# Gates' logits in four parts and sinkhorn's steps in another order, in a kernel of delta-rule attention, a Mish layer and a sinkhorn-gated expert layer

## The chip, the core and the metric

The kernel runs on one core of a Trainium2 chip. The core has TensorE (matmuls, with a sequence of weight loads beside them), VectorE, ScalarE, GpSimd and SyncE (which issues the DMAs here); in profiles they are PE, PEld, DVE, ACT, POOL and SP. Each works off its own queue in order, and semaphores tie the queues together. PSUM holds matmul results, SBUF the rest.

The metric is the device time of one execution in microseconds, as a median of runs. The median before is 2372.52 us (three runs, 2372.46 to 2373.16).

## The reference, cut to what matters

```python
def _moe2_ref(x, w_gate, w1, w2):              # x: 3072 tokens of 384
    logits = x @ w_gate                        # 8 experts
    logits = logits - logits.max()
    P = np.exp(logits)
    for _ in range(8):                         # sinkhorn
        P /= P.sum(1, keepdims=True) + 1e-09
        P /= P.sum(0, keepdims=True) + 1e-09
        P *= N / E
    for e in range(E):
        h = np.maximum(x @ w1[e], 0.0)         # 384 -> 1024
        ye = h @ w2[e]                         # 1024 -> 384
        out += P[:, e:e + 1] * ye
```

Ahead of it stand a delta-rule attention over 768 positions (`y[t] = q[t] S`, then a rank-1 update of S for each of 32 heads) and a layer of 2048 hidden units with the Mish activation. All is float32; the large matmuls are done in three passes of split operands (high x high, high x low, low x high).

## The kernel before, in words

**First stage.** Tokens come in six blocks (c = 0 to 5) of 512. In each block, 16 units of the Mish layer are followed by 8 units of expert 0: `for f in range(U1, NU)`, f = 16 to 23, called s16 to s23. Meanwhile the attention of the next blocks is spread over the units by a table (`PLACES`, `window`), and its elimination steps on VectorE are handed out by `fill` and by `tick`, which runs behind every operation called through `vec` (all of these have line 458 in the profile).

**Second stage.** Experts 1 to 7 go over the six blocks in units of 128 hidden features, block 5 first (`for u in range(N1, N + 2)`; unit v = u - N1 counts from 0).

**A unit.** `e_first` is the first matmul of a unit: nine 512-column matmuls into a PSUM tile `psh`. `e_relu` makes two SBUF tiles of it: `hh` (ScalarE, relu of `psh`) and `hl` (VectorE, what `hh` lost in rounding). `e_second` (called by `y0_second` and `o_second`) multiplies them with the second weights, twelve 384-column matmuls, and runs two units behind its `e_first`. `hh` and `hl` have two buffers each, so the `hh` of a unit can be written when the `e_second` of the unit two before has read its own. In the first stage `e_relu(u - 1)` is called in unit u, in the second stage `e_relu(u)`.

**Weights.** `conversions` splits the next weights: a ScalarE copy (line 251) and a GpSimd subtraction (line 252), at the end of a unit. Every sixth unit of the second stage, from v = 3, `x2_split` does the same with a block's tokens (lines 1189 and 1190).

**Gates.** `logits(c)` multiplies a block's tokens `xr` with the gates' weights: 4 token tiles x 3 products in float32, recorded as 24 matmuls of 8 columns, and one VectorE copy into `lg`. It is called in unit s17, in the last block in s16.

**Sinkhorn.** `lg` holds all logits, then P, as 128 x 24 x 8. `sink_start` finds the maximum over partitions by a transpose and a product on TensorE and takes exp by way of a sigmoid. `sink_round` is five VectorE operations (lines 352 to 356): row sums, + 1e-9, reciprocal, multiply, column sums over the 24. `sink_round_end` is a product with a matrix of ones on TensorE (line 360), which adds the column sums over the partitions, and four VectorE operations (lines 362 to 365): + 1e-9, reciprocal, scale, multiply. `sink_step` takes the next one of a list of 18 (`sinks`). In the last block it is called twice a unit from s17 on, ahead of `e_second` and behind it; in the second stage once between `e_first` and `e_relu` and once behind `e_second`. Units 0 and 1 of the second stage take the last four steps. The PSUM tiles of these products come from `bank()`, two buffers that the second stage's odd units share. When the list is empty, `P` scales the accumulators of expert 0, one tile a unit (line 1251).

The order on every engine is that of the code (`manual_schedule`).

Of the kernel before, what the change touches and what calls it, by code (L numbers as in the profile page):

```python
# [13 lines left out]
ALU = mybir.AluOpType  # L14
# [70 lines left out]
def delta_mish_sinkhorn_kernel(  # L85
# [246 lines left out]
    P = lg  # L332
    Pf = lg.rearrange("p t e -> p (t e)")

    def sink_start():
        m1, m2, m3 = sk["m"][:, 0:1], sk["m"][0:1, 1:2], sk["m"][:, 2:3]
        nc.vector.tensor_reduce(out=m1, in_=Pf, axis=AX.X, op=ALU.max)
        ps = small[0]()
        nc.tensor.transpose(ps[0:1, 0:128], m1, id_sb)
        nc.vector.tensor_reduce(out=m2, in_=ps[0:1, 0:128], axis=AX.X, op=ALU.max, negate=True)  # L340
        ps2 = small[0]()[:, 0:1]
        mm(ps2, lhsT=sk["ones"][0:1, :], rhs=m2, start=True, stop=True)
        nc.vector.tensor_copy(m3, ps2)
        nc.scalar.activation(out=Pf, in_=Pf, func=AF.Sigmoid, bias=m3)
        d = sk["d"]
        nc.vector.tensor_scalar(out=d, in0=Pf, scalar1=-1.0, scalar2=1.0, op0=ALU.mult, op1=ALU.add)
        nc.vector.reciprocal(out=d, in_=d)
        nc.vector.tensor_tensor(out=Pf, in0=Pf, in1=d, op=ALU.mult)
# [15 lines left out]
        nc.vector.tensor_scalar(out=cr, in0=cr, scalar1=float(NTOK) / E, scalar2=None, op0=ALU.mult)  # L364
        nc.vector.tensor_tensor(out=P, in0=P, in1=cr[:, None, :].to_broadcast([128, NT, E]), op=ALU.mult)

    sinks = deque([sink_start, lambda: None] + [sink_round, sink_round_end] * ROUNDS)

    def sink_step():
        if sinks:  # L370
            sinks.popleft()()
# [6 lines left out]
    with ExitStack() as p1:  # L378
# [474 lines left out]
            if c < NBLK - 1:  # L853
                nc.sync.dma_start(out=x2_dram[c], in_=xr)

        def logits(c):
            ps = bank()[:, 0:4 * E].rearrange("p (t e) -> p t e", e=E)
            for t in range(4):
                for k in range(KD):
                    mm(ps[:, t, :], lhsT=xr[:, k, t * 128:(t + 1) * 128], rhs=wg_sb[:, k, :], start=(k == 0), stop=(k == KD - 1))  # L860
            vec.tensor_copy(lg[:, 4 * c:4 * c + 4, :], ps)


        def fill(us):
# [175 lines left out]
        def window(c):  # L1040

            pe = {m: [] for m in MARKS}
            rest = {m: [] for m in MARKS}
            late = {m: [] for m in MARKS}
            nxt, far = c + 1, c + 2
            rest[f"s{U1 + (c < NBLK - 1)}"].append(lambda: logits(c))
            if c == 0:
                for t in (2, 3):
                    pe["s1"].append(lambda t=t: st_s(0, t))
                for t in range(4):  # L1050
                    rest[f"s{t + 1}"].append(lambda t=t: prep_v(1, t))
                for i in range(8):
                    rest[f"s{i + 2}"].append(lambda t=i // 2, w=1 + i % 2: mask_p(1, t, (w,)))
            if nxt < NBLK:
                m0, at = PLACES[c][0:2]
                rest[MARKS[m0]].append(drain_elim if c else lambda: elim1(60, nc.vector))
                rest[MARKS[m0]].append(lambda: st_lane_out(nxt))
                for hf in range(2):
                    late[MARKS[m0 + 1]].append(lambda hf=hf: st_m1(nxt, hf))
                    rest[MARKS[m0 + 2]].append(lambda hf=hf: st_place(nxt, hf, (0, 2)))  # L1060
                    late[MARKS[m0 + 2]].append(lambda hf=hf: st_m2(nxt, hf))
                ch = chain_list(nxt)
                assert len(at) >= len(ch)
                for p, stage in zip(at, ch):
                    pe[MARKS[p]].append(stage)
            if far < NBLK:
                sq0, mb0, at, kq0, kt0, eq0 = PLACES[c][2:]
                if c == 0:
                    rest["s2"].append(lambda: load_kt(far))
                    rest["s2"].append(lambda: load_vt(far))  # L1070
                if far + 1 < NBLK:
                    rest[MARKS[kt0]].append(lambda: load_kt(far + 1))
                    rest[MARKS[kt0]].append(lambda: load_vt(far + 1))
                for t in range(4):
                    rest[MARKS[sq0 + t // 2]].append(lambda t=t: prep_sq(far, t))
                rest[MARKS[sq0 + 1]].append(lambda: prep_pow(far, ALL))
                rest[MARKS[sq0 + 3]].append(lambda: [op() for op in norm_ops(far, ALL)])
                rest[MARKS[kq0]].append(drain_decode)
                for t in range(4):
                    rest[MARKS[kq0]].append(lambda t=t: load_kq(far, t))  # L1080
                    rest[MARKS[mb0[t]]].append(lambda t=t: prep_mb(far, t, nc.gpsimd))
                    for hf in range(2):
                        pe[MARKS[at[2 * t + hf]]].append(lambda t=t, hf=hf: st_g(far, t, hf, True))
                    rest[f"s{U1 + t + 4}"].append(lambda t=t: prep_v(far, t))
                rest[MARKS[eq0]].append(lambda: eq.extend(lane_in_ops(far) + elim_ops(far)))
            return pe, rest, late

        with tc.manual_schedule():
            banks[:] = [0, [A1, A1]]
            for c in range(NBLK):  # L1090
# [50 lines left out]
                for f in range(U1, NU):  # L1141
                    u = b + f
                    posts = side_pe(f"s{f}", 0)
                    ready(u)
                    e_first(u, ps_h, mi_p, x1h, x1l)
                    if f > U1:
                        e_relu(u - 1)
                    side_rest(f"s{f}", posts)
                    if f > U1:
                        fill(3.6 if c == 0 else 3.2)  # L1150
                    if c == NBLK - 1 and f > U1:
                        sink_step()
                    if f > U1 + 1:
                        y0_second(u - 2)
                    if c == NBLK - 1 and f > U1:
                        sink_step()
                    conversions(u)
                e_relu(b + NU - 1)
                split = [lambda kc=kc: st_x1(c + 1, kc) for kc in range(KD)] if c + 1 < NBLK else []
# [58 lines left out]
    with tc.manual_schedule():  # L1218
# [10 lines left out]
        for u in range(N1, N + 2):  # L1229
            v = u - N1  # L1230
            if u < N:
                e, c, f = info(u)
                e_first(u, *[(ps_h, mi_p), (ps_a, mi_p)][v % 2], *xs[c], *[("h",), ("a",)][v % 2])
                sink_step()
                e_relu(u)
            if v >= 2:
                o_second(u - 2)
            sink_step()
            if u < N:
                conversions(u)  # L1240
            if v >= 3 and (v - 3) % 6 == 0 and (v - 3) // 6 < NBLK - 1:
                c = (v - 3) // 6
                x2_split(c)
                if c + 2 < NBLK - 1:
                    x2_load(c + 2)
                if c + 1 < NBLK - 1:
                    acc_load(c + 1)
            if not sinks and todo:
                c, t = todo.popleft()
                a = acc[c][:, t, :]  # L1250
                nc.vector.tensor_scalar(out=a, in0=a, scalar1=P[:, 4 * c + t, 0:1], scalar2=None, op0=ALU.mult)
# [63 lines left out]
```

## Time and profile before

| | |
|---|---|
| median of three runs | 2372.52 us |
| the profiled execution, whole | 2370.98 us |
| its span, first to last instruction | 2369.2 us |
| TensorE busy | 2298.2 us, 97% of the span |
| VectorE, ScalarE, GpSimd busy | 34%, 24%, 20% |
| granted TensorE clock, mean | 0.971 of full speed |

Busy shares are an average over unlike stages. The first stage ends and the second begins at 949.6 us; sinkhorn runs from 914.8 to 959.0 us. In the second stage TensorE is busy without a break from 964 us to the end. What a change there is worth is read from the stretch itself: which wait of TensorE ends last, and at which clock its matmuls run.

### The profile page before, as it was taken

Reading aid. Unit: us, or ns where it says so; the run is one execution under the profiler, and the core shown is the slowest. Engines: PE = TensorE matmul, PEld = TensorE weight load, DVE = VectorE, ACT = ScalarE, POOL = GpSimd, SP = SyncE. Lnnn points to the kernel's source line nnn. Section 1 sums busy time; section 2 is a strip of 40 time slices with the busy share of each in tenths; the row PEclk is TensorE's granted clock in tenths of the full one; section 3 lists DMA queues with packets and bytes.
Section 4 is the critical chain, followed back from the end, with each engine's and each line's share of the span. In section 5 each row is a group of like instructions: output and inputs, shape, how many; then the busy total and the mean of one; then the engine's idle time right before and its main releaser. Section 6 shows DMA issues by size and latency. Waiting matters only on the chain.

```text
span 2369.2 us, 36112 instructions
## 1 busy us (share of the span) xinstructions
PE 2298.2 (97%) x15492; PEld 1992.1 (84%) x15492; DVE 801.2 (34%) x1369; ACT 559.9 (24%) x999; POOL 471.2 (20%) x370
## 2 busy tenths in 40 slices
PE   8688899999999999999999999999999999999998
PEld 4477778878788888899999999999999999999998
DVE  8884725527162104431222222222222122212222
ACT  5244332332323232211211211121121111112111
POOL 5686442341412121310200100020020011001000
PEclk6799999999999999999999999999999999999999
DMA  5357643637344454410100100010010001000111
GB/s 173 134 195 211 211 154 129 211 114 238 131 164 148 162 198 140 167 40 1 54 1 1 37 17 1 1 54 1 1 54 1 1 20 34 1 1 27 27 27 27
DMA packets 79727, 196.00 MB, mean 83 GB/s; under 512 B 7696, under 2 KB 50448, under 8 KB 79568
## 3 DMA queue, kind: packets, MB, share of 16 engines
q1 hardware_dynamic: 79568, 193.70, 24.8%
q8 instruction: 122, 2.00, 0.3%
q14 instruction: 37, 0.30, 0.0%
HBM read 161.43 MB, written 32.24 MB: 82 GB/s over the span
## 4 chain that ended last, share of the span: by engine, by line
PE 90%; DVE 6%; DMA 2%; POOL 1%; issue 1%; ACT 0%; SPq 0%; DVEq 0%; POOLq 0%; ACTq 0%
PE psh L299 42%; PE o L321 30%; PE x L840 8%; PE y L321 3%; DVE t L635 1%; DVE lane L641 1%; PE psa L590 1%; PE psa L729 1%; PE psa L763 1%; DVE lane L623 1%; PE psa L711 1%; PE psa L860 1%; PE psa L747 1%; PE psa L677 1%; DMA wd<-w 0%
## 5 line engine op out<-in xcount | busy, mean ns | idle before, releaser
L299 PE MATMUL psh<-xh,w 128*128 128x512 f32 x2052 | 662.7, 404 | 13.7 <-DMA w<-wd 6.7
L314 DVE SCALAR_TENSOR_TENSOR hl<-psh,hh 128x512 fp32r<-128x512 f32 x384 | 265.1, 690 | 1111.8 <-ACT hh L313 1111.7
L313 ACT ACTIVATE hh<-psh 128x512 fp32r<-128x512 f32 x384 | 229.7, 598 | 1312.1 <-PE o L321 1154.5
L299 PEld LDWEIGHTS psh<-xh,w 128*128 128x128 f32 x2052 | 381.1, 191 | 91.2 <-issue 12.2
L299 PE MATMUL psh<-xl,w 128*128 128x512 f32 x1026 | 412.0, 402 | 4.2 <-DVE xl L458 4.2
L321 PE MATMUL o<-w,hh 128*128 128x384 f32 x1584 | 405.5, 337 | 0.0
L321 PEld LDWEIGHTS o<-w,hh 128*128 128x128 f32 x1584 | 288.2, 188 | 19.8 <-issue 4.9
L321 PE MATMUL o<-wx,hh 128*128 128x384 f32 x1104 | 282.0, 336 | 0.0
L321 PE MATMUL o<-w,hl 128*128 128x384 f32 x792 | 267.0, 337 | 0.0
L299 PE MATMUL psh<-xh,wx 128*128 128x512 f32 x828 | 258.3, 393 | 0.0
L299 PEld LDWEIGHTS psh<-xl,w 128*128 128x128 f32 x1026 | 196.3, 191 | 51.2 <-DVE xl L458 5.9
L321 PEld LDWEIGHTS o<-wx,hh 128*128 128x128 f32 x1104 | 201.5, 188 | 13.1 <-issue 2.1
L829 POOL TENSOR_TENSOR gl<-x,gh 128x512 fp32r<-128x512 f32 x96 | 127.5, 1328 | 420.0 <-ACT gh L828 416.2
L252 POOL TENSOR_TENSOR w<-raw,w 128x768 fp32r<-128x768 f32 x41 | 75.7, 1848 | 669.9 <-ACT w L251 669.8
L321 PE MATMUL o<-wx,hl 128*128 128x384 f32 x552 | 186.0, 337 | 0.0
L299 PEld LDWEIGHTS psh<-xh,wx 128*128 128x128 f32 x828 | 153.5, 188 | 25.2
L299 PE MATMUL psh<-xl,wx 128*128 128x512 f32 x414 | 163.4, 395 | 0.0
L840 PE MATMUL x<-gh,w 128*128 128x512 f32 x576 | 150.7, 397 | 0.0
L321 PEld LDWEIGHTS o<-w,hl 128*128 128x128 f32 x792 | 148.6, 188 | 0.0
L840 PEld LDWEIGHTS x<-gh,w 128*128 128x128 f32 x576 | 107.5, 189 | 24.9
L252 POOL TENSOR_TENSOR wx<-raw,wx 128x768 fp32r<-128x768 f32 x23 | 42.4, 1845 | 399.7 <-ACT wx L251 399.7
L321 PEld LDWEIGHTS o<-wx,hl 128*128 128x128 f32 x552 | 103.6, 188 | 0.0
(165 smaller groups left out, 2358.2 us busy)
## 6 DMA issues: line engine op xcount, KB each, us to landing
w<-wd SPq DMA_DIRECT2D x120, 768.0 KB, 4.4
raw<-in_w_dram SPq DMA_DIRECT2D x128, 192.0 KB, 2.6
wd<-w SPq DMA_DIRECT2D x24, 768.0 KB, 4.3
kq<-in_qkb_dram SPq DMA_DIRECT2D x20, 256.0 KB, 6.9
vt<-in_vtok_dram SPq DMA_DIRECT2D x6, 768.0 KB, 8.6
kq<-in_w_in_dram SPq DMA_DIRECT2D x12, 384.0 KB, 4.7
kq<-in_w_out_dram SPq DMA_DIRECT2D x12, 384.0 KB, 5.6
y0d<-xr SPq DMA_DIRECT2D x6, 768.0 KB, 4.7
```

The lines of the kernel that those rows point to most:

```text
L252: nc.gpsimd.tensor_tensor(out=w[:, 1], in0=r, in1=w[:, 0].bitcast(F32), op=ALU.subtract)
L299: mm(ps, lhsT=wi(u, pw, kc), rhs=(xh, xl)[px][:, kc, :], start=(n == 0), stop=(n == 3 * KD - 1))
L313: nc.scalar.activation(out=h, in_=ps, func=AF.Relu)
L314: nc.vector.scalar_tensor_tensor(out=l, in0=ps, scalar=0.0, in1=h.bitcast(F32), op0=ALU.max, op1=ALU.subtract)
L321: mm(o[t], lhsT=(h, l)[ph][:, t * 128:(t + 1) * 128], rhs=wo(u, pw, 0, DM), start=(f == 0 and n == 0), stop=(f == U2 - 1 and n == 2))
L590: mm(ps[0:64, :, i], lhsT=k[64:64 + D, 0, h, :], rhs=k[64:64 + D, 0:2, h, :], start=True, stop=True)
L623: + [(1.14, lambda p=p: nc.vector.transpose(out=lane[p:p + 32], in_=v[p:p + 32, 32:64, :])) for p in (32, 96)]
L635: eng[0].tensor_tensor(out=slot[0], in0=lane[:, s + 1:32, s:s + 1].to_broadcast([128, n, s]), in1=lane[:, s:s + 1, 0:s].to_broadcast([128, ...
L641: eng[0].tensor_tensor(out=lane[:, s + 1:32, 0:s], in0=lane[:, s + 1:32, 0:s], in1=slot[0], op=ALU.add)
L677: mm(ps[p + 32:p + 64, i], lhsT=g[p:p + 32, t, h, 32:64], rhs=t11[p:p + 32, b, :], start=True, stop=True)
L829: nc.gpsimd.tensor_tensor(out=l, in0=p, in1=h.bitcast(F32), op=ALU.subtract)
L840: mm(x2ps[c][k], lhsT=wo(u, pw, k * 128, k * 128 + 128), rhs=(h, l)[pg], start=(f == 0 and n == 0), stop=(f == U1 - 1 and n == 2))
```

## The change

Two things are changed.

`logits` takes a token tile t and makes one of four parts: 6 of the 24 matmuls, into a PSUM tile of its own, and a copy of 8 columns. The parts are called in four units in a row, s17 to s20, in the last block s16 to s19.

The list of steps has 22 entries: the local maximum, the transpose with the maximum over partitions, and the rest of the start are steps of their own, with empty steps between. `sink_step` is called twice in a row, in the last block from s19 on, ahead of `e_second`; in the second stage behind `e_relu` and ahead of `e_second`. With that a unit holds the end of one round and then the next round's sums, and the product with the ones stands a unit behind the sums that it reads. Two rounds are ended in the last block, six in units 0 to 5 of the second stage.

```diff
+    def sink_max():
+        nc.vector.tensor_reduce(out=sk["m"][:, 0:1], in_=Pf, axis=AX.X, op=ALU.max)
+
+    def sink_max_all():
+        ps = small[0]()
+        nc.tensor.transpose(ps[0:1, 0:128], sk["m"][:, 0:1], id_sb)
+        nc.vector.tensor_reduce(out=sk["m"][0:1, 1:2], in_=ps[0:1, 0:128], axis=AX.X, op=ALU.max, negate=True)
+
     def sink_start():
-        m1, m2, m3 = sk["m"][:, 0:1], sk["m"][0:1, 1:2], sk["m"][:, 2:3]
-        nc.vector.tensor_reduce(out=m1, in_=Pf, axis=AX.X, op=ALU.max)
-        ps = small[0]()
-        nc.tensor.transpose(ps[0:1, 0:128], m1, id_sb)
-        nc.vector.tensor_reduce(out=m2, in_=ps[0:1, 0:128], axis=AX.X, op=ALU.max, negate=True)
+        m2, m3 = sk["m"][0:1, 1:2], sk["m"][:, 2:3]
...
-    sinks = deque([sink_start, lambda: None] + [sink_round, sink_round_end] * ROUNDS)
+    none = lambda: None
+    sinks = deque([sink_max, none, sink_max_all, none, sink_start] + [sink_round, sink_round_end] * ROUNDS + [none])
...
-        def logits(c):
-            ps = bank()[:, 0:4 * E].rearrange("p (t e) -> p t e", e=E)
-            for t in range(4):
-                for k in range(KD):
-                    mm(ps[:, t, :], lhsT=xr[:, k, t * 128:(t + 1) * 128], rhs=wg_sb[:, k, :], start=(k == 0), stop=(k == KD - 1))
-            vec.tensor_copy(lg[:, 4 * c:4 * c + 4, :], ps)
+        def logits(c, t):
+            ps = bank()[:, 0:E]
+            for k in range(KD):
+                mm(ps, lhsT=xr[:, k, t * 128:(t + 1) * 128], rhs=wg_sb[:, k, :], start=(k == 0), stop=(k == KD - 1))
+            vec.tensor_copy(lg[:, 4 * c + t, :], ps)
...
-            rest[f"s{U1 + (c < NBLK - 1)}"].append(lambda: logits(c))
+            for t in range(4):
+                rest[f"s{U1 + (c < NBLK - 1) + t}"].append(lambda t=t: logits(c, t))
...
-                    if c == NBLK - 1 and f > U1:
+                    if c == NBLK - 1 and f > U1 + 2:
+                        sink_step()
                         sink_step()
                     if f > U1 + 1:
                         y0_second(u - 2)
-                    if c == NBLK - 1 and f > U1:
-                        sink_step()
...
+                e_relu(u)
                 sink_step()
-                e_relu(u)
+                sink_step()
             if v >= 2:
                 o_second(u - 2)
-            sink_step()
```

VectorE's queue in the second stage. Before, from the end of round 7 in unit 0 on (the round with its line 356, then `hl` of unit 1, then the end of round 8):

```order
L365 TENSOR_TENSOR lg<-lg,gate 128x192
L352 TENSOR_REDUCE gate<-lg 128x24
L353 TENSOR_SCALAR gate<-gate 128x24
L354 RECIPROCAL gate<-gate 128x24
L355 TENSOR_TENSOR lg<-lg,gate 128x192
L356 TENSOR_REDUCE gate<-lg 128x8
L314 SCALAR_TENSOR_TENSOR hl<-psh,hh 128x512
L362 TENSOR_SCALAR gate<-psa 128x8
L363 RECIPROCAL gate<-gate 128x8
L364 TENSOR_SCALAR gate<-gate 128x8
```

After, unit 2 of the second stage, between the last row of unit 1 and the first of unit 3 (the lines are four higher: 360 is the column sums, 366 to 369 the end of a round):

```order
L360 TENSOR_REDUCE gate<-lg 128x8
L314 SCALAR_TENSOR_TENSOR hl<-psh,hh 128x512
L366 TENSOR_SCALAR gate<-psa 128x8
L367 RECIPROCAL gate<-gate 128x8
L368 TENSOR_SCALAR gate<-gate 128x8
L369 TENSOR_TENSOR lg<-lg,gate 128x192
L356 TENSOR_REDUCE gate<-lg 128x24
L357 TENSOR_SCALAR gate<-gate 128x24
L358 RECIPROCAL gate<-gate 128x24
L359 TENSOR_TENSOR lg<-lg,gate 128x192
L360 TENSOR_REDUCE gate<-lg 128x8
L314 SCALAR_TENSOR_TENSOR hl<-psh,hh 128x512
```

Before, the round stood ahead of its unit's `hl`; now `hl` comes first, then the end of the round before, then the next round.

TensorE's queue in the second stage, unit 3. Before, `e_first` (`psh`) is followed by `e_second` (`o`):

```order
L299 MATMUL psh<-xl_1199,wx_8591 128x512
L299 MATMUL psh<-xh_1198,wx_8591 128x512 x2
L299 MATMUL psh<-xl_1199,wx_8591 128x512
L321 MATMUL o_8694<-w_86,hh 128x384 x2
L321 MATMUL o_8694<-w_86,hl 128x384
```

After, at the same place, with the product with the ones (`gate`) between them:

```order
L299 MATMUL psh<-xl_1199,wx_8588 128x512
L299 MATMUL psh<-xh_1198,wx_8588 128x512 x2
L299 MATMUL psh<-xl_1199,wx_8588 128x512
L364 MATMUL psa<-gate 128x8
L321 MATMUL o_8701<-w_86,hh 128x384 x2
L321 MATMUL o_8701<-w_86,hl 128x384
```

Before, units 0 and 1 alone had such a product, behind their `e_first`; now units 0 to 5 have one, and from unit 2 on it stands ahead of an `e_second`.

TensorE's queue in block 4, units s17 to s18, the logits (`psa<-wg_sb,xr`). Before:

```order
L299 MATMUL psh<-xh_1198,w_1200 128x512 x2
L299 MATMUL psh<-xl_1199,w_1200 128x512
L860 MATMUL psa<-wg_sb,xr 128x8 x12
L299 MATMUL psh<-xh_1198,w_85 128x512 x2
L299 MATMUL psh<-xl_1199,w_85 128x512
```

After, from the same matmul on:

```order
L299 MATMUL psh<-xh_1198,w_1200 128x512 x2
L299 MATMUL psh<-xl_1199,w_1200 128x512
L865 MATMUL psa<-wg_sb,xr 128x8 x3
L299 MATMUL psh<-xh_1198,w_85 128x512 x2
L299 MATMUL psh<-xl_1199,w_85 128x512
L299 MATMUL psh<-xh_1198,w_85 128x512 x2
L299 MATMUL psh<-xl_1199,w_85 128x512
L299 MATMUL psh<-xh_1198,w_85 128x512 x2
L299 MATMUL psh<-xl_1199,w_85 128x512
L865 MATMUL psa<-wg_sb,xr 128x8 x3
L321 MATMUL y_7650<-w_89,hh 128x384 x2
```

The lump of twelve products is now three, and three more follow behind each of the next three units' `e_first`.

## Rows read from the trace of the kernel before

**Rows 1.** TensorE's timeline, second stage: start us, us, line, operation, tiles, shape, count, [idle].
```profile
957.34 0.60 PE L360 MATMUL psa<-gate 128*128 128x8 f32 x2 [3.16 <-DVE gate L356]
957.79 1.20 PE L299 MATMUL psh<-xh,w 128*128 128x512 f32 x2
...
961.33 0.52 PE L321 MATMUL o<-w,hh 128*128 128x384 f32 x2
...
963.43 0.63 PE L299 MATMUL psh<-xh,wx 128*128 128x512 f32 x2
...
965.53 0.51 PE L321 MATMUL o<-w,hh 128*128 128x384 f32 x2
```

**Rows 2.** Timeline of TensorE, last block: products of sinkhorn's start and first round.
```profile
916.70 0.38 PE L342 MATMUL psa<-gate 1*128 1x1 f32 x2 [0.37 <-DVE gate L340]
...
922.23 0.39 PE L360 MATMUL psa<-gate 128*128 128x8 f32 x2 [0.75 <-DVE gate L356]
```

**Rows 3.** Waits of TensorE's weight loads, 900 to 965 us: total us, times, longest.
```profile
PEld psa L360 <- DVE gate L356: 5.4, 4, 3.6
```

**Rows 4.** Stretches: from:to, length, each engine's busy us (count), PEclk, DMA share, GB/s.
```profile
237.14:243.97 6.83, 6.83 (x36) 5.63 (x33) 1.17 (x3) 2.35 (x5) 5.03 (x7) 0.50 0.58 175
...
810.56:813.97 3.41, 3.41 (x11) 3.02 (x10) 0.00 (x0) 0.00 (x0) 0.00 (x0) 0.50 0.92 386
913.88:917.00 3.12, 2.75 (x14) 1.96 (x13) 1.32 (x4) 0.00 (x0) 0.00 (x0) 1.00 0.00 0
957.36:960.77 3.41, 3.41 (x9) 2.83 (x10) 1.85 (x6) 0.00 (x0) 1.07 (x1) 0.50 1.00 401
```

**Rows 5.** Timeline of TensorE, block 4: the logits and units beside them.
```profile
806.63 2.74 PE L860 MATMUL psa<-wg_sb,xr 128*128 128x8 f32 x24
809.22 0.71 PE L299 MATMUL psh<-xh,w 128*128 128x512 f32 x2
...
815.06 0.63 PE L299 MATMUL psh<-xh,w 128*128 128x512 f32 x2
```

**Rows 6.** Timeline of VectorE, block 1: the copy of the logits.
```profile
397.14 0.19 DVE L458 COPY lg<-psa 128x32 f32<-128x32 f32 x1 [3.25 <-PE psa L860]
```

**Rows 7.** Timeline of TensorE, block 1: second unit after the logits.
```profile
403.30 0.73 PE L299 MATMUL psh<-xh,w 128*128 128x512 f32 x2 [0.34 <-DVE hl L314]
```

**Rows 8.** Timeline of ScalarE, second stage.
```profile
963.46 0.60 ACT L313 ACTIVATE hh<-psh 128x512 fp32r<-128x512 f32 x1 [7.64 <-PE o L321]
965.54 0.85 ACT L251 ACTIVATE wx<-raw 128x768 fp32r<-128x768 f32 x1 [1.48 <-DMA raw<-in_w_dram]
```

**Rows 9.** Timeline of VectorE, last block and second stage.
```profile
920.35 0.34 DVE L352 TENSOR_REDUCE gate<-lg 128x24 f32<-128x192 f32 x1
...
953.12 0.15 DVE L362 TENSOR_SCALAR gate<-psa 128x8 f32<-128x8 f32 x1
...
954.14 0.35 DVE L352 TENSOR_REDUCE gate<-lg 128x24 f32<-128x192 f32 x1
...
955.08 1.68 DVE L355 TENSOR_TENSOR lg<-lg,gate 128x192 f32<-128x192 f32 x1
...
964.09 0.69 DVE L314 SCALAR_TENSOR_TENSOR hl<-psh,hh 128x512 fp32r<-128x512 f32 x1 [3.48 <-ACT hh L313]
964.70 0.41 DVE L1251 TENSOR_SCALAR acc<-acc,lg 128x384 f32<-128x384 f32 x1
...
973.06 1.64 DVE L1251 TENSOR_SCALAR acc<-acc,lg 128x384 f32<-128x384 f32 x1
```

**Rows 10.** VectorE's operations on lg: count, ns min/median/max, first, last start.
```profile
L355 DVE TENSOR_TENSOR lg<-lg,gate x8: 357/358/1675, 921.3 to 955.1; 128x192 f32<-128x192 f32 x8
```

**Rows 11.** Timeline of GpSimd, second stage.
```profile
954.74 3.69 POOL L252 TENSOR_TENSOR wx<-raw,wx 128x768 fp32r<-128x768 f32 x2 [11.07 <-ACT wx L251]
...
969.05 1.96 POOL L252 TENSOR_TENSOR wx<-raw,wx 128x768 fp32r<-128x768 f32 x1 [0.73 <-ACT wx L251]
970.96 3.52 POOL L1190 TENSOR_TENSOR xl<-x2r,xh 128x1536 fp32r<-128x1536 f32 x1
```

## The prediction, made before the changed kernel ran

> **What bounds the kernel now.** I read TensorE's timeline first. In the second stage a unit is one `e_first` (nine 512-column matmuls), 965.53 - 963.43 = 2.10 us, and one `e_second`, 963.43 - 961.33 = 2.10 us, back to back: 4.20 us with TensorE never idle [rows 1]. So a microsecond that TensorE loses is lost, and what other engines do counts only where TensorE waits for it or where its clock falls. The change touches two places where that happens. The first are sinkhorn's products with the ones matrix, which wait for VectorE's column sums: 0.75 us at 922.23 in the last block and 3.16 us at 957.34 in the second stage [rows 1, 2]; the waits of their weight loads come to 5.4 us, 3.6 of them at 957.34, and the product after the maximum adds 0.37 us [rows 2, 3]. The second is the clock: granted at 0.50 of full speed (1.2 instead of 2.4 GHz) for 6.83 us after the logits of block 0, for 3.41 us after those of block 4, and for 3.41 us after the 3.16 us wait; after the logits of block 5 it stayed at 1.00 [rows 4].
>
> **Logits in four parts.** The 24 matmuls of 8 columns take 809.22 - 806.63 = 2.59 us in a lump; a part is a quarter, 0.65 us, and the four sum to the same. What can change is the clock behind them and who waits for whom.
> Block 4: from the end of the lump to the end of the unit's `e_second` pass 815.06 - 809.22 = 5.84 us, where a unit takes 4.20 [rows 5]. Nothing waits there, so the clock costs 1.64 us. Parts of 0.65 us, each amid 4.2 us of full matmuls, should not lower it: -1.6 us.
> Blocks 1 to 3 are different. VectorE sits idle for 3.25 us until the logits come, copies them at 397.14, then works off elimination steps, and `hl` behind them releases TensorE only at 403.30, after a wait of 0.34 us [rows 6, 7]. That is 6.2 us behind the copy, against 4.20 of matmuls, so the clock there costs nothing. With the split the copy of the first part lands 1.94 us sooner and so does 403.30; the second part lies in TensorE's wait, the third and fourth cost 0.65 us each. 1.94 - 1.30 = 0.65 us a block, -1.9 us in three.
> Block 0: 6.83 us at half clock, 3.4 us lost at most, but the chunks' small matmuls stand there too and can lower the clock by themselves: between 0 and -3.4, I take -1.6. Together **-5.1 us**, bounds 0 and -10 (the latter if the third and fourth parts were hidden too).
>
> **The sinkhorn steps.** The products keep their number (eight, plus two for the maximum). New is the order: in every unit `e_relu`, then the product and VectorE's four operations of a round's end, then the next round's five. The product of a unit needs the sums that VectorE made in the unit ahead. In the last block that works: `e_relu` there serves the unit before, whose buffers are free at the unit's start. In the second stage, to which six products now fall instead of two, `e_relu` serves the unit itself, and it is now ahead of the round in VectorE's queue. Its ScalarE half `hh` waits for the buffer that `e_second` of two units before still reads: it starts at 963.46, 0.03 us after that `e_second` is over at 963.43, having waited 7.64 us [rows 1, 8]. VectorE's `hl` follows at 964.09 and the next operation in its queue at 964.70 [rows 9]. So behind the end of a unit come: 1.27 us to the end of `hl`; the four operations, 954.14 - 953.12 = 1.02; the five to the product, 922.23 - 920.35 = 1.88 [rows 2, 9]. The sums are there 4.17 us into the next unit, and TensorE wants them after its `e_first`, at 2.10. **Each product of the second stage whose predecessor unit had an `e_second` waits at least 2.07 us.** Queued behind it on TensorE is the `e_second`, and with that the buffer for the next `hh`, so nothing catches up.
> GpSimd makes this longer. The weight conversions put a subtraction of 1.9 us on it, and VectorE operations that read only SBUF are held until it ends: the round's multiply at 955.08 took 1.68 us where the median of the eight is 0.358 [rows 9, 10], while the GpSimd operations begun at 954.74 ran [rows 11]; the scale of an accumulator at 973.06 took until 974.70, and GpSimd's 3.52 us from 970.96 end at 974.48 [rows 9, 11]. The multiply of a round's end works on the same tiles, `lg` and `gate`, so I take it to be held as well; `hl`, which reads PSUM, I take to be free. The Trainium skill ("SBUF — State Buffer", section "Who interferes with whom") has the rule behind it: a VectorE instruction with two SBUF inputs is blocked for the whole of a GpSimd instruction that reads SBUF, if that began first. By that rule the multiply of a round's end is held too, which no run of it shows; without it the sum below is about 1 us less, as the next multiply is held in its stead.
> Unit by unit:
> Last block, unit 22 (first round's product): from the product of the maximum to the first sums pass 922.23 - 916.70 = 5.53 us, less one `hl` of 0.61: 4.92 [rows 2, 9]. TensorE covers two halves of 2.10 and the product of some 0.3, 4.5: a wait of 0.4 us. But two conversions are queued on ScalarE right behind the sigmoid, and their GpSimd operations can hold two of VectorE's for up to 1.96 each: between 0.4 and 4.3, I take 2.7, since the first is met part way.
> Second stage, unit 1: the same order and the same GpSimd operation as now at 955.08, so the 3.16 us and the low clock stay: 0. Unit 2: the sums come about 3.5 us behind the product of unit 1, and `e_first` at the low clock takes 961.33 - 957.79 = 3.54 [rows 1]: 0; at full clock a wait of 1.0 would replace the 1.44 us of clock.
> Unit 3: the conversion waits for its weights until 965.54, 2.1 us into its unit [rows 8]; with 0.85 for the copy GpSimd runs from about 3.0 to 4.9 and holds the round's multiply, so the sums come at 5.7: wait 3.6.
> Unit 4: GpSimd starts 1.42 us into the unit (969.05, where the unit starts at 965.53 + 2.10 = 967.63), and right behind it runs the 3.52 us split, to 6.9 [rows 11]. The third operation of the end (at about 1.7) is held to 3.4, the fourth by the split to 6.9, then 0.2 and 1.88: 9.0, wait 6.9.
> Unit 5: one conversion: third operation held to 3.4, sums at 5.9, wait 3.8.
> New waits: 2.7 + 3.6 + 6.9 + 3.8 = 17.0. Clock: after 3.16 us of idling `e_first` took 3.54 instead of 2.10, 1.44 lost [rows 1, 4]; three of the new waits are longer, the one of 2.7 I count half: 3.5 x 1.44 = 5.0. Gone are the waits of the last block, 5.4 - 3.6 + 0.4 = 2.2 [rows 2, 3]. Sum **+19.8 us**. Bounds: +6 (GpSimd's holds half as long, the clock never falling) to +23.
> Later work: the accumulators' scaling starts four units later and still ends a unit ahead of the first sum into each. SP's queue and DMA issues are unchanged.
>
> **Sum.** 19.8 - 5.1 = +14.7 us. The profiled execution took 2370.98 us (span 2369.2), 1.54 under the median of 2372.52; 2370.98 + 14.7 = 2385.7 by the profile, **2387.2 us** by the median.
>
> **Rivals.** (a) GpSimd's operations miss VectorE's. Then the waits are 0.4 and three times 2.07, unit 2 waits 1.0, unit 1 only 2.07 instead of 3.16 and the clock stays up (-1.44): 0.4 + 6.2 + 1.0 - 1.1 - 1.4 - 2.2 - 5.1 = -2.2, 2370.3 us. For it: half a microsecond of shift can let an operation slip through. Against it: the conversions come in every unit from 0 to 5, behind the same `hh` as VectorE's work. 10%.
> (b) The change does what it says and no product waits: -(3.16 + 1.44 + 2.2 + 5.1) = -11.9, 2360.6 us. It needs `hl` not to stand ahead of the round, or `hh` not to wait for `e_second`; the orders and [rows 8] say both do. 3%. It decides if the sums come less than 2.10 us into a unit.
> (c) The lump of logits never cost any clock, the low stretches have another cause and stay. Then 1.6 + 1.6 us of the gain go: 2390.4 us. 5%. The Trainium skill ("TensorE: Matmul & The Clock Gate", section "HAM oscillation — how this bites in real kernels") ties the fall to idle gaps of TensorE, and the lump has none; the 0.50 behind it in two blocks [rows 4] speaks against that reading.
> (d) In blocks 1 to 3 three more copies, each with an elimination step called behind it, delay `hl`: 0.6 us in nine units and 1.44 us of clock in three, +9.7: 2396.9 us. Against it: a unit with a logits part is 4.85 us long, enough for the 0.6 us more. 10%.
>
> **How the numbers follow.** The forecast, with its bounds mostly between 2378 and 2394, has 72%; (a) 10, (b) 3, (c) 5, (d) 10. The range 2377 to 2395 holds the forecast, (c) and the milder half of (d). Measurements here tell 0.2%, 4.7 us, from no change: slower than 2377.3 are the forecast, (c), (d): 87%; within are (a)'s: 10%; faster (b)'s: 3%.
>
> **What would show it.** In the profile after: products of the second stage waiting for VectorE in units 1, 3, 4 and 5 (3.2, 3.6, 6.9, 3.8 us), none after; `hl` ahead of a round each time; multiplies held 1.5 to 3.5 us; granted clock 0.50 behind these waits and 1.00 behind the logits of block 4; blocks 1 to 3 shorter by 0.65 us each. It is wrong if `hh` starts ahead of the end of `e_second`, or if the waits stay near 2 us.

## The result and the profile after

The changed kernel takes **2389.77 us** (median of six executions, 2384.70 to 2399.84), the kernel before 2372.32 us beside it (six, 2370.71 to 2373.16). The ratio is 1.0078, 95% interval 1.0057 to 1.0100: slower by more than the noise, where 2387.2 was forecast in a range of 2377 to 2395. The profiled execution of the changed kernel, 2384.70 us (span 2382.6), was the fastest of its six, so the traces are 13.7 us apart and the medians 17.5.

TensorE's timeline of the changed kernel, all products that wait, from the last block (932.47) to unit 5 of the second stage (986.85), answers [rows 1, 2]:

```profile
932.47 0.39 PE L364 MATMUL psa<-gate 128*128 128x8 f32 x2 [2.40 <-DVE gate L360]
...
952.81 0.39 PE L364 MATMUL psa<-gate 128*128 128x8 f32 x2 [3.16 <-DVE gate L360]
...
956.25 0.39 PE L364 MATMUL psa<-gate 128*128 128x8 f32 x2 [0.85 <-DVE gate L360]
...
964.29 0.39 PE L364 MATMUL psa<-gate 128*128 128x8 f32 x2 [3.37 <-DVE gate L360]
...
976.93 0.60 PE L364 MATMUL psa<-gate 128*128 128x8 f32 x2 [6.41 <-DVE gate L360]
...
986.85 0.39 PE L364 MATMUL psa<-gate 128*128 128x8 f32 x2 [2.98 <-DVE gate L360]
```

The waits of the same products between 900 and 1000 us (total, times, longest) answer [rows 3]:

```profile
PEld psa L364 <- DVE gate L360: 21.8, 6, 6.8
PE psa L364 <- DVE gate L360: 19.2, 6, 6.4
```

What makes unit 4's 6.41 us long stands in three timelines, which answer [rows 8, 9, 11]. ScalarE's, `hh` of that unit:

```profile
968.19 0.60 ACT L313 ACTIVATE hh<-psh 128x512 fp32r<-128x512 f32 x1 [6.58 <-PE o L321]
```

VectorE's, the multiply of unit 3's round, then `hl` of unit 4 and the end of a round behind it:

```profile
961.89 1.81 DVE L359 TENSOR_TENSOR lg<-lg,gate 128x192 f32<-128x192 f32 x1
...
968.82 0.69 DVE L314 SCALAR_TENSOR_TENSOR hl<-psh,hh 128x512 fp32r<-128x512 f32 x1 [4.58 <-ACT hh L313]
...
969.85 1.60 DVE L368 TENSOR_SCALAR gate<-gate 128x8 f32<-128x8 f32 x1
971.49 3.53 DVE L369 TENSOR_TENSOR lg<-lg,gate 128x192 f32<-128x192 f32 x1
```

GpSimd's, a conversion's subtraction and the split's:

```profile
969.60 1.82 POOL L252 TENSOR_TENSOR wx<-raw,wx 128x768 fp32r<-128x768 f32 x1 [6.11 <-ACT wx L251]
971.37 3.42 POOL L1195 TENSOR_TENSOR xl<-x2r,xh 128x1536 fp32r<-128x1536 f32 x1
```

`hh` starts when the `e_second` before is over, `hl` follows, and behind `hl` the scale of the column sums ends as GpSimd's first subtraction does, at 971.4, and the multiply as the second does, at 974.8 to 975.0. The Trainium skill ("SBUF — State Buffer", section "Who interferes with whom") has a VectorE instruction with two SBUF inputs wait for the whole of such a GpSimd instruction; the 3.53 us of the multiply, 0.36 elsewhere, agree.

TensorE's granted clock in five stretches of the changed kernel (columns as in [rows 4]), behind the waits of 2.40, 3.16 and 0.85, 3.37, 6.41 and 2.98 us:

```profile
934.14:937.56 3.42, 3.42 (x11) 3.03 (x10) 2.21 (x6) 1.33 (x2) 0.60 (x1) 0.50 0.00 0
952.81:958.66 5.85, 5.00 (x25) 4.24 (x26) 3.11 (x10) 0.00 (x0) 1.10 (x1) 1.00 1.00 407
964.80:968.20 3.40, 3.40 (x12) 3.40 (x12) 0.00 (x0) 0.01 (x1) 0.00 (x0) 0.50 0.34 108
975.10:981.90 6.80, 4.97 (x16) 4.88 (x17) 1.63 (x5) 0.62 (x2) 0.00 (x0) 0.50 0.61 231
986.80:990.20 3.40, 3.35 (x18) 3.19 (x19) 0.26 (x1) 0.89 (x2) 0.00 (x0) 1.00 0.06 23
```

The clock fell behind three of the waits and not behind the other two places.

Two unit starts on TensorE bound each stretch below; they are the same in every kernel. From the last block's unit 16 to unit 11 of the second stage the kernel before took 88.07 us and the changed one 107.04: **+18.97 us for the steps**. From unit 16 to unit 23 the five other blocks took 170.29 and 167.15 together: **-3.14 for the logits** in this pair of profiles. What is left to 13.7, -2.1 us, lies mainly ahead of unit 16 of the blocks, in units that the change does not touch.

### The profile page after: what moved, and what is told of

The parts are those of the page before. It is cut to its first block, busy times and chain, and to the rows that moved or that the text cites. A ratio compares the mean times of both kernels' runs of the same rounds, so it can differ in the third digit from the quotient of the medians.

```text
span 2382.6 us, 36144 instructions
## 1 busy us (share of the span) xinstructions
PE 2292.7 (96%) x15492; PEld 1987.9 (83%) x15492; DVE 810.5 (34%) x1387; ACT 560.2 (24%) x999; POOL 470.6 (20%) x370
## 4 chain that ended last, share of the span: by engine, by line
PE 89%; DVE 6%; DMA 1%; POOL 1%; issue 1%; ACT 0%; SPq 0%; DVEq 0%; POOLq 0%; ACTq 0%
PE psh L299 41%; PE o L321 30%; PE x L846 8%; PE y L321 4%; DVE t L641 1%; DVE lane L647 1%; PE psa L735 1%; PE psa L596 1%; PE psa L769 1%; PE psa L717 1%; DVE lane L629 1%; PE psa L753 1%; PE psa L683 1%; PE psa L865 0%; DMA w<-wd 0%
```

## The experiments

### The two halves apart

`e1_split` has the kernel before's steps, and the logits in parts in blocks 0 to 4:

```diff
-            rest[f"s{U1 + (c < NBLK - 1)}"].append(lambda: logits(c))
+            if c == NBLK - 1:
+                rest[f"s{U1}"].append(lambda: logits(c))
+            for t in range(4 if c < NBLK - 1 else 0):
+                rest[f"s{U1 + 1 + t}"].append(lambda t=t: logits_part(c, t))
...
```

> The kernel before with the logits in four parts in blocks 0 to 4 (block 5 keeps its lump, since sinkhorn's start there needs all logits in s16); sinkhorn's steps as before. Theory: the parts alone bring what the profile of the change shows up to block 5, unit 16, -5.7 us: about 2366.6 us against 2372.3; block 4 runs its units behind the first part at the full clock (4.2 + 0.65 us instead of 5.84), blocks 1 to 3 gain about 0.65 us each because VectorE's queue sets the end there. Rival: the gain up to block 5 belongs to something else (the run, not the parts), and the time stays within 1.5 us of before.

Measured: 2371.95 us, ratio 1.0000 (0.9991 to 1.0009) to the kernel before. `e2_steps` is the changed kernel with the logits in a lump again:

> The changed kernel with the logits in one lump as before: sinkhorn's steps in the new order alone. Theory: the loss is the steps' alone, +19 to +24 us over before, 2391 to 2396 us, with waits of the products of 2.4, 3.2, 0.9, 3.4, 6.4 and 3.0 us in the last block and units 1 to 5 of the second stage. Rival: the split of the logits is part of the loss in the median runs, and without it the time is below that of the change.

Measured: 2392.63 us, ratio 1.0088 (1.0071 to 1.0105), and 108.95 us from unit 16 to unit 11. The steps alone cost 20 us, as expected. The parts alone gave nothing that the times show, where 5 to 6 us were expected. A second profile of the changed kernel:

> The changed kernel once more, for its spread from run to run (2384.7 to 2399.8 in six runs, where before spreads over 2.5). Theory: the waits are the same in every run, and the clock falls behind a different number of them: the profile shows the same six waits within 1 us, and a time above 2385 goes with more stretches at 0.50 between 930 and 1000 us. Rival: the waits themselves change with the landing of the weights, and a slower run shows a longer wait in unit 3 or 4.

2388.26 us, ratio 1.0067 (1.0053 to 1.0081); its profile has waits of 2.40, 3.15, 3.22, 6.50 and 3.19 us and 107.31 us from unit 16 to unit 11. These five repeat to some 0.2 us. Unit 2's 0.85 is missing: this time the clock fell behind unit 1's wait, so `e_first` took longer and covered it. The clock fell in four places of the stretch here and in three in the first profile, and the stretch is 0.3 us longer; what makes the 7.4 us between the two executions lies ahead of it.

The times tell little of the parts. With the old steps they are worth 0.7 us (2371.95 against 2372.67), with the new ones 4.4 (2388.26 against 2392.63, five and four executions), and the units ahead of the logits, which neither changes, differ by more than that from execution to execution (see the last section). So the parts are read from stretches below.

### Why the parts gave so little

All profiles of this study that share a stretch can be set side by side. Unit 16 to unit 23, us (three kernels' profiles with a lump in every block: before, `e2_steps`, `e8_before_again`; seven with parts in blocks 0 to 4: the changed kernel, `e1_split` and `e3_relu_behind` to `e7_split_later`):

| block | lump, three profiles | mean | parts, lowest to highest | mean | difference | forecast |
|---|---|---|---|---|---|---|
| 0 | 49.75, 49.62, 48.61 | 49.33 | 47.72 to 48.42 | 48.02 | -1.3 | -1.6 |
| 1 | 30.58, 30.46, 30.18 | 30.41 | 29.44 to 30.02 | 29.53 | -0.9 | -0.65 |
| 2 | 30.12, 30.12, 30.11 | 30.12 | 30.66 to 32.59 | 31.09 | **+1.0** | -0.65 |
| 3 | 30.12, 30.12, 30.16 | 30.13 | 30.65 to 31.03 | 30.77 | **+0.6** | -0.65 |
| 4 | 29.73, 29.74, 28.21 | 29.23 | 28.16 to 28.19 | 28.17 | -1.1 | -1.6 |
| sum | | 169.2 | | 167.6 | **-1.6** | -5.1 |

Blocks 2 and 3 went the other way. VectorE's copy of the logits in the kernel before, blocks 2 and 3, had much less idle time ahead of it than block 1's 3.25 us [rows 6]:

```profile
536.72 0.19 DVE L458 COPY lg<-psa 128x32 f32<-128x32 f32 x1 [0.71 <-PE psa L860]
...
680.01 0.19 DVE L458 COPY lg<-psa 128x32 f32<-128x32 f32 x1 [0.70 <-PE psa L860]
```

In the changed kernel, block 2, VectorE is still at its transposes when the first part is done, and TensorE waits for the `hl` behind them. VectorE's timeline there:

```profile
530.00 1.95 DVE L629 STREAM_TRANSPOSE lane<-gx 32x1024 f32<-32x1024 f32 x1
531.98 0.69 DVE L314 SCALAR_TENSOR_TENSOR hl<-psh,hh 128x512 fp32r<-128x512 f32 x1
```

TensorE's timeline there, the first part and the unit after it:

```profile
530.61 0.73 PE L865 MATMUL psa<-wg_sb,xr 128*128 128x8 f32 x6
532.73 0.73 PE L299 MATMUL psh<-xh,w 128*128 128x512 f32 x2 [1.39 <-DVE hl L314]
```

So 1.39 of the 1.94 us that the shorter first part saves are a wait, and the third and fourth part still cost 0.65 each. TensorE has this wait, 1.38 or 1.39 us long, in blocks 2 and 3 of all seven profiles. In six of them the clock also fell behind it in one of the two blocks (in the changed kernel for 3.4 us from 674.7 on, in block 3): such a block took 31.0 us, 32.59 in `e7_split_later`, where the others took 30.7. Next, the kernel before again:

> The kernel before, once more, for its profile. If a lump of logits lowers the clock whenever it is run, the stretches at 0.50 stand again behind the lumps of the same blocks (at about 237, 397, 537, 680 and 810 us), and the one behind the 3.16 us wait of the second stage at 957. If the clock falls there by chance, one or more of the five is missing or a new one stands elsewhere, and the span differs from 2369.2 us by 1.4 us for each.

2371.81 us. The clock fell at the lumps of blocks 0, 1 and 2, not at those of 3 and 4. Two stretches of that profile, at block 4's lump and at block 3's:

```profile
807.65:815.00 7.35, 7.35 (x49) 6.85 (x47) 0.79 (x2) 1.04 (x2) 0.00 (x0) 1.00 0.96 363
680.97:684.40 3.43, 3.43 (x18) 3.02 (x18) 3.17 (x8) 0.00 (x0) 0.00 (x0) 1.00 1.01 405
```

Block 4 then took 28.21 us, as with parts, and block 3 took 30.16 at full clock and 30.12 at the low one: there the clock costs nothing, as the prediction had it. `e11_split_three` has the kernel before's steps, parts in blocks 0, 1 and 4, a lump in 2, 3 and 5:

```diff
+            if c in (2, 3, NBLK - 1):
+                rest[f"s{U1 + (c < NBLK - 1)}"].append(lambda: logits(c))
+            for t in range(4 if c in (0, 1, 4) else 0):
...
```

> The kernel before, with its steps, and the logits in parts in blocks 0, 1 and 4 only; blocks 2, 3 and 5 in a lump. Theory (the parts gain where VectorE idles ahead of the copy or where the clock falls behind the lump, and cost two times 0.65 us where VectorE is busy until 0.7 us ahead of the copy): units 16 to 23 take 47.9, 29.5, 30.1, 30.1 and 28.2 us in blocks 0 to 4, 165.8 together, 3.4 less than the mean of 169.2 of the lumps, and the time is 3 us under the kernel before (where parts in five blocks gave -0.7). Rival (what the profiles show ahead of block 5 is lost again behind it, in clock): blocks as above, and no difference in the median.

Measured: 47.81, 29.46, 30.14, 30.12 and 28.18 us, 165.7 together, as the theory said; the time is 2369.75 us, ratio 0.9994 (0.9985 to 1.0003), as the rival said. In its profile and in `e1_split`'s the clock fell at block 5's lump, where it stayed up in the kernel before [rows 4], in `e8_before_again` and in `e2_steps`. That stretch of `e1_split`:

```profile
909.82:913.24 3.42, 3.42 (x10) 2.66 (x10) 1.05 (x3) 0.00 (x0) 0.00 (x0) 0.50 0.00 0
```

And of `e11_split_three`:

```profile
905.81:916.05 10.24, 9.87 (x27) 7.53 (x27) 4.77 (x12) 0.94 (x2) 0.00 (x0) 0.50 0.02 8
```

From unit 16 to 22 block 5 took 28.84 and 30.72 us there, against 27.30 and 27.31 in the two profiles of the kernel before. That gives back 1.5 and 3.4 us of a gain of 2 to 3.5. Whether block 5's lump pays more often when lumps ahead of it are split, or by chance twice, five profiles cannot tell; it stays open.

### What the waits are made of

`e3_relu_behind` is the changed kernel with `hl` behind the steps:

```diff
-                e_relu(u)
                 sink_step()
                 sink_step()
+                e_relu(u)
```

> The changed kernel with one line moved: in the second stage e_relu behind the two steps, so that VectorE has the round's end and the next round ahead of hl. Theory (hl, waiting for hh and with it for e_second, holds the round up): the sums come about 1 to 2 us into the next unit, the waits in units 3 and 5 go, in unit 4 one of about 2.6 us stays (two GpSimd operations in a row), units 1 and 2, which have no e_second to cover the steps, keep 1 to 3.5 us each. About 10 us less than the change: 2376 to 2383 us. Rival (GpSimd's holds alone make the waits, the place of hl does not matter): the waits stay as they are, 2385 to 2395 us.

Measured: 2380.54 us, ratio 1.0028 (1.0015 to 1.0040); 97.15 us from unit 16 to unit 11, 9.9 less than the changed kernel. All its products that still wait:

```profile
940.10 0.60 PE L364 MATMUL psa<-gate 128*128 128x8 f32 x2 [2.40 <-DVE gate L360]
...
957.98 0.39 PE L364 MATMUL psa<-gate 128*128 128x8 f32 x2 [0.74 <-DVE gate L360]
963.53 0.39 PE L364 MATMUL psa<-gate 128*128 128x8 f32 x2 [2.96 <-DVE gate L360]
...
981.91 0.60 PE L364 MATMUL psa<-gate 128*128 128x8 f32 x2 [3.30 <-DVE gate L360]
```

Those of units 3 and 4 are gone, unit 1's is 0.74 instead of 3.16; unit 2 has 2.96 and unit 5, behind the split, 3.30, which I had looked for in unit 4. The place of `hl` is half of the loss. `e5_no_hold` takes GpSimd away instead:

```diff
-        nc.gpsimd.tensor_tensor(out=w[:, 1], in0=r, in1=w[:, 0].bitcast(F32), op=ALU.subtract)
+        if quiet[0]:
+            nc.scalar.activation(out=w[:, 1], in_=r, func=AF.Copy, scale=0.0)
+        else:
+            nc.gpsimd.tensor_tensor(out=w[:, 1], in0=r, in1=w[:, 0].bitcast(F32), op=ALU.subtract)
...
```

> The changed kernel, but while sinkhorn's steps run (last block from unit 19 on, second stage units 0 to 5, and the first split of tokens) GpSimd's subtraction is replaced by a ScalarE write of zeros. This leaves out the low halves of the weights of those units and of one block's tokens; the number of matmuls stays the same. Theory (GpSimd's subtractions hold VectorE's SBUF-only operations, and that is what the waits have above 2.1 us): the waits of the products, 2.40, 3.16, 0.85, 3.37, 6.41, 2.98 us in the changed kernel, become about 0.5 (last block), 2.0 (unit 1), 1.0 (unit 2) and 2.1 (units 3, 4 and 5), and the round's multiplies all take about 0.36 us; some 9 us of waits go, with up to two low-clock stretches of 1.44 us: 9 to 12 us less than the changed kernel, about 2377 to 2380 us. Rival (the excess comes from VectorE's own queue or from late weights): the waits of units 3 and 4 stay at 3.4 and 6.4, the time within 3 us of the changed kernel's 2388.

Measured: 2373.54 us, ratio 1.0015 (1.0004 to 1.0025); 94.46 us, 12.6 less than the changed kernel. Its products in the last block and in units 1, 3, 4 and 5, from TensorE's timeline:

```profile
937.30 0.39 PE L369 MATMUL psa<-gate 128*128 128x8 f32 x2 [0.31 <-DVE gate L365]
...
954.79 0.39 PE L369 MATMUL psa<-gate 128*128 128x8 f32 x2 [1.85 <-DVE gate L365]
...
965.48 0.39 PE L369 MATMUL psa<-gate 128*128 128x8 f32 x2 [1.92 <-DVE gate L365]
973.07 0.39 PE L369 MATMUL psa<-gate 128*128 128x8 f32 x2 [1.36 <-DVE gate L365]
979.65 0.39 PE L369 MATMUL psa<-gate 128*128 128x8 f32 x2 [1.91 <-DVE gate L365]
```

Its multiplies between 930 and 985 us, grouped by line (count, ns min/median/max, first and last start):

```profile
L364 DVE TENSOR_TENSOR lg<-lg,gate x8: 357/358/360, 936.3 to 978.7; 128x192 f32<-128x192 f32 x8
...
L374 DVE TENSOR_TENSOR lg<-lg,gate x7: 359/360/360, 938.4 to 977.4; 128x192 f32<-128x192 f32 x7
```

No multiply is held any more, and some 1.9 us of the waits in units 1, 3 and 5 stay, and 1.36 in unit 4, whose `e_first` ran in part at the low clock. So a wait of the second stage is about 2 us from `hl` ahead of the round (2.07 forecast) and the rest from holds; either one taken away removes half of the loss or more, so the two do not simply add. `e7_split_later` moves the tokens' split from unit 3 to unit 6 (`v >= 6 and (v - 6) % 6 == 0`):

> The changed kernel with one edit: the split of a block's tokens (ScalarE copy and GpSimd subtraction of 3.5 us) comes in unit 6, 12, ... instead of 3, 9, ..., so that it is behind sinkhorn's last round. Theory (unit 4's wait of 6.41 us is the conversion's hold plus the split's): that wait falls to that of its neighbours, 3.0 to 3.4 us, the others stay, and the time is 3 to 3.5 us less than the changed kernel's (4 to 5 if a low-clock stretch goes too). Rival (the long wait has another cause, such as the wait in the unit before): 6 us stay in unit 4, and the time is the same within 1 us.

Unit 4's wait fell to 3.33 us, as expected, but the time is 2388.72 us. The split now came too late for the next block of tokens, and TensorE's timeline shows what took the place:

```profile
1003.68 0.75 PE L299 MATMUL psh<-xl,w 128*128 128x512 f32 x1 [2.04 <-POOL xl L1195]
```

Besides, the clock fell in five places instead of three.

### A version that beats both

`e6_all_behind` puts the steps where neither cause reaches them:

```diff
-... sink_max_all, none, sink_start] + [sink_round, sink_round_end] * ROUNDS + [none])
+... sink_max_all, none, sink_start, none, none] + [sink_round, sink_round_end] * ROUNDS + [none])
...
-                e_relu(u)
-                sink_step()
-                sink_step()
+                if v >= 2:
+                    sink_step()
+                    sink_step()
+                e_relu(u)
...
-            if v >= 3 and (v - 3) % 6 == 0 and (v - 3) // 6 < NBLK - 1:
+            if v >= 6 and (v - 6) % 6 == 0 and (v - 6) // 6 < NBLK - 1:
...
```

> The changed kernel with what the waits are put down to taken away by place, with nothing left out: the two steps stand ahead of e_relu in the second stage, two more empty steps put the first round a unit later, no steps are taken in units 0 and 1 of the second stage (units 2 to 8 take them), the split of tokens starts at unit 6 instead of 3, and unit 8 scales four accumulators at once. Theory (the waits come from hl ahead of the steps in VectorE's queue, and from GpSimd's subtractions and split): a unit of 4.2 us lies between a round's sums and their product, of which VectorE needs some 3 us, or 5 with one hold, so products wait under 1 us each; the tail (from block 5's unit 22 to the end) is 2 to 7 us shorter than in the kernel before instead of 19 longer, and with 0 to -5 for the logits the time is 2361 to 2370 us. Rival (a product so far from its sums waits as long as the holds last, wherever hl stands): waits of 2 to 3 us stay in each of the seven units, and the time is 2380 or more.

2369.52 us, ratio 0.9995 (0.9985 to 1.0004): the 19 us are gone, but nothing is gained. From unit 16 to unit 11 it takes 88.11 us, and two waits above 0.3 us are left:

```profile
966.49 0.39 PE L364 MATMUL psa<-gate 128*128 128x8 f32 x2 [1.75 <-DVE gate L360]
...
981.62 0.50 PE L299 MATMUL psh<-xl,w 128*128 128x512 f32 x1 [1.72 <-POOL xl L1195]
```

The second is `e7_split_later`'s mistake again. The first goes back to ScalarE, where `hh` stood behind a weight conversion that had waited 6.70 us for its DMA, with four loads of 768 KB queued ahead. The next two versions keep this order, load tokens and accumulators later (in units 3 and 6, or in unit 2), have the logits in a lump in blocks 2 and 3, and split the tokens in unit 1 (`e9_split_first`) or 5 (`e10_split_five`):

> The version with all steps ahead of e_relu, and with what its trace showed taken away: the tokens' first split in unit 1 of the second stage (it came too late, TensorE waited 1.72 us for it), the loads of tokens and accumulators for later blocks in units 3 and 6 instead of ahead of unit 0 (weights came 6.7 us after ScalarE asked for them, and with them hh, the round and the product of unit 5, 1.75 us and a low clock), and the logits in a lump in blocks 2 and 3 and in parts in the others. Theory: the stretch from block 5's unit 16 to the second stage's unit 11 takes 81 to 84 us instead of 88.1 (both in the kernel before and in the version so far); blocks 2 and 3 are back at 30.12 us from unit 16 to 23, the five blocks together at 166 to 167 instead of 169.2; the time is 6 to 9 us under the kernel before. Rival (GpSimd's subtractions hold the steps wherever the split stands): a wait of 2 to 3 us appears in unit 3 or 4 in place of the one removed, and the stretch stays at 86 to 88.

> The same with the tokens' first split in unit 5, amid the steps, instead of unit 1. Theory: its subtraction of 3.5 us holds the last operation of a round's end in unit 6, so the product behind it waits 2 to 3 us, with 1.4 us if the clock falls: 2 to 4.5 us more than with the split in unit 1. Rival (the steps' unit of slack absorbs a hold of 3.5 us): the two are the same within 1 us.

Measured: 2366.40 us, ratio 0.9979 (0.9968 to 0.9989), 86.96 us with the split in unit 1; 2363.33 us, 0.9966 (0.9954 to 0.9979), 84.90 us with the split in unit 5. I had them in the wrong order: with the split in unit 1 the wait moved to unit 3 (956.65, 3.13 us) and the clock fell, as the rival said. The version with the split in unit 5 has these two:

```profile
974.95 0.50 PE L299 MATMUL psh<-xl,w 128*128 128x512 f32 x1 [0.62 <-POOL xl L1204]
...
978.82 0.39 PE L364 MATMUL psa<-gate 128*128 128x8 f32 x2 [1.99 <-DVE gate L360]
```

`e12_split_thirds` cuts that split into three:

```diff
+            if 3 <= v <= 5:
+                x2_split(0, slice(v - 3, v - 2))
...
```

> The version with the tokens' first split in unit 5, but that split in three parts of 512 columns, one each in units 3, 4 and 5. In the version with one split its subtraction of 3.49 us and the conversion's of 1.83 right behind it held two of VectorE's operations for 2.49 and 1.95 us, the product of unit 8 waited 1.99 us, and TensorE waited 0.62 us for the split's result. Theory (what counts is how long one hold is against the slack of a unit): parts of about 1.2 us hold for 1.2 us at most each, the wait of 1.99 falls under 0.5 and that of 0.62 goes; the stretch from block 5's unit 16 to unit 11 of the second stage takes 82.3 to 83 us instead of 84.9, and the time is about 2 us less than with one split, 2360 to 2362 us against 2371 of the kernel before. Rival (the sum of the holds counts, not the longest): a product waits 1.5 to 2 us in another unit, and the stretch stays at 84 to 85.

Measured: **2362.36 us, ratio 0.9960 (0.9946 to 0.9974)** to the kernel before, and 82.86 us from unit 16 to unit 11. No wait of TensorE in the steps is above 0.30 us, and the granted clock stays at 1.00 from 688 to 2363 us. By stretches, the gain over the kernel before is 5.2 us here (88.07) and some 3.2 in blocks 0 to 4 (166.05 against 169.2). Three of VectorE's rows there; held operations come in most units, none longer than 1.98 us:

```profile
965.33 1.40 DVE L369 TENSOR_TENSOR lg<-lg,gate 128x192 f32<-128x192 f32 x1
...
969.94 1.40 DVE L369 TENSOR_TENSOR lg<-lg,gate 128x192 f32<-128x192 f32 x1
...
975.75 1.98 DVE L359 TENSOR_TENSOR lg<-lg,gate 128x192 f32<-128x192 f32 x1
```

What counts is how long one round is held against the slack of a unit, not the sum of all holds. Sinkhorn's operations between 925 and 992 us, each beyond the shortest of its kind, lost 9.2 us to holds in this version and 8.4 in the one with the split in unit 5, where two in one round (2.49 and 1.95 us long) made the wait of 1.99. Between the last two versions the medians (2363.33 and 2362.36) tell no difference, the stretches (84.90 and 82.86) do.

## Why the prediction was right, and where it was off

**The steps, +19.8 forecast: right.** One pair of profiles has +18.97, and `e2_steps` has +20.0 in the median (2392.63 against 2372.67). By terms, forecast and measured: last block 2.7 and 2.40; unit 1 3.16 and 3.16; unit 3 3.6 and 3.37; unit 4 6.9 and 6.41; unit 5 3.8 and 2.98. Unit 2 took the second of the two ways that the prediction named: the clock stayed up behind unit 1's wait, so 0.85 us of waiting (1.0 forecast) came in place of 1.44 of clock. Unit 5's wait was put 0.8 too high: its sums came 5.4 us into the unit, not 5.9, and its `e_first`, begun at the low clock, took 2.5. The stretch from unit 16 to 22, -2.2 forecast, became 24.65 instead of 27.30 us: -2.65, of which 0.8 only moved, as four products of some 0.2 us now stand behind unit 22. From there on it is +21.62: new waits 16.0 (17.0 forecast), the four products 0.9, which leaves 4.7 for the clock (5.0 forecast). The clock's total is near the forecast by luck: 3.5 more falls were counted, and there were two more, one of which lasted 6.8 us instead of 3.4. `e3_relu_behind` and `e5_no_hold` show both causes apart.

**The logits, -5.1 forecast: the failed step.** Blocks 0, 1 and 4 came out at -3.2 together (-3.85 forecast). The step that failed is the one for blocks 1 to 3: "VectorE sits idle for 3.25 us until the logits come" was read in block 1 and taken three times. Blocks 2 and 3 show 0.71 and 0.70 us at the same place, in the same trace; their parts cost 1.6 us instead of gaining 1.3. Block 4's -1.6 rested on one execution in which the clock had fallen; in a second one it had not. With -1.6 us for the logits and +18.97 for the steps the sum is +17.4, where +14.7 was forecast and the medians are 17.5 apart: the logits were 3.5 us off one way and the steps 0.8 the other. That sum and medians agree to 0.1 is luck too, as the six executions lie 15 us apart. The forecast's place in its range is owed to the steps, which outweigh the logits.

**The rivals.** (a), GpSimd missing VectorE, was put at 2370.3 us, 2.2 under the median before; `e5_no_hold`, which forces it, came 3.7 over the kernel before beside it (2369.88). Of the gap of 5.9 the logits are 3.5; for the rest, (a) let the clock stay up, and it fell behind three of the waits there. (b), no product waiting, was put 11.9 us under; `e12_split_thirds`, where none does by more than 0.30 us, but which moves loads and the split too, is 10.2 under (2372.56 beside it). (c) is half true: a low clock follows the lump in some executions only, and the parts got low stretches of their own in blocks 2 and 3. The Trainium skill ("TensorE: Matmul & The Clock Gate", section "HAM oscillation — how this bites in real kernels") ties the fall to idle gaps; the 0.50 behind a lump without a gap, in two kernels' block 5 too, does not agree. (d) had the right blocks in part, but the delay there is VectorE's transposes, not the added copies.

## What to carry to other kernels

Before a step is moved, find its place in each in-order queue relative to the operation that frees the bottleneck's buffers: here a round's five operations, 1.88 us, put behind an `hl`, cost 20 us together with GpSimd's holds, and saved 1.9 us of waits. Where a figure is used for several blocks, look up the row of each block; the same table of work had 3.25 us of slack in one and 0.7 in two. A long GpSimd operation beside small VectorE work on a due date is cheaper in pieces shorter than the slack of one unit, by 2 us of the stretch here.

## What the runs showed of the hardware that I had not expected

The same lump of matmuls was followed by a granted clock of 0.50 in one execution and of 1.00 in another of the same kernel (block 4: [rows 4] and 807.65:815.00 above); block 5's had 1.00 in the kernel before, and 0.50 for 3.42 and 10.24 us in two others. The clock fell behind a wait of 2.40 us (934.14) and stayed at 1.00 behind one of 3.16 (952.81), which in the kernel before had been followed by 0.50 [rows 4], and was so in the second profile of the changed kernel too. In `e5_no_hold` it fell behind waits of 1.85, 1.92 and 1.91 us and not behind one of 1.36, in `e1_split` and others behind one of 1.38 or 1.39. A VectorE operation on 128x8 elements, 0.17 us elsewhere, took 1.60 beside a GpSimd subtraction. Units 0 to 15 of blocks 1 to 5 took between 478.6 and 488.9 us from profile to profile, and 478.6 and 484.0 in two of the changed kernel itself: 5.4 of the 7.4 us between those two executions.
